# Decay tiles loaded as two 64-partition transfers, with new planner costs and due times, in a fused chunked-scan and gated-FFN kernel

## The chip, the cores and the metric

The kernel runs on one core of a Trainium2 chip. The metric is the time of one execution in device microseconds. Five engines work side by side, each through its own queue in order: TensorE (PE, with its weight loads shown apart as PEld), VectorE (DVE), ScalarE (ACT), GpSimd (POOL) and SyncE (SP). Here SP only issues transfers: each DMA instruction on its queue starts a transfer between HBM and the on-chip memories, and the transfers are carried by 16 DMA engines.

## The reference

A state-space scan in chunks, followed by a gated feed-forward layer over its output:

```python
# x: (4 batches, 8 heads, 768 steps, 32); a: (4, 8, 768); B, C: (4, 8, 768, 16)
for c in range(nc):                       # chunks of the sequence
    la  = log(clip(a, 1e-6, 1))[chunk];  cum = cumsum(la)
    L   = exp(cum_i - cum_j) for i >= j, else 0
    CB  = C_i . B_j
    y   = (CB * L) @ x  +  (C @ state) * exp(cum)
    state = exp(sum(la)) * state + sum_j exp(cum_last - cum_j) * B_j x_j^T
x2 = y as (3072 tokens, 256)
out = (sigmoid(x2 @ w_gate) * (x2 @ w_val)) @ w_out      # 256 -> 1536 -> 256
```

## The kernel before, in words

The sequence is cut into six chunks of 128 steps (c = 0 to 5), each worked as two halves of 64. A *unit* is one chunk of one batch (b = 0 to 3), so there are 24 units, numbered u = 4c + b, and they are worked two at a time from c = 1 on. When the four units of a chunk are done, its 512 tokens go through the feed-forward layer: 12 blocks f of 128 hidden columns, each a gate product `pg` and a value product `pv` (`gate`, `value`), then four output products `po` (`proj`). Chunk 0 uses the weights whole, in fp32; for chunks 1 to 5 the weights (18 tiles `w0` to `w17`) and the activations are each split into a rounded high part and a low part, and three products of parts stand for one.

What a unit does, by the names in the profile:

- `bn`, `cn`, `xn`: its B, C and x. Two transposes `pt` on PE give `bct`.
- `ab`, 128 partitions x 512 columns: its decays. Partition rows 0 to 63 all hold the same 512 values, those of the first half of the chunk (8 heads x 64 steps), and rows 64 to 127 those of the second half. They come out of a DRAM scratch `a_z`, in which the clipped `a` was saved with the first step of each half set to zero (`save_z`, L853). From c = 1 on `load_a` (L267) fetches them; a scan on DVE (L409, `decays`) turns them into the products of decays. In chunk 0 they are spread by PE instead (L569, `spread`).
- `pp`: the running products of `a`, from a second scratch `a_p` (`load_p`, L273).
- `weigh` (L468) multiplies the products C.B in PSUM (`pcb`, made by `multiply`, L454) by the decays and gives `m`; `within` (L480, L487) multiplies `m` by x; the state goes on through `ml`, `sm` (L522), `mr`, `sn` (L441) on DVE, and PE adds the part of the earlier state (L531). ACT and DVE then store the output of the unit as two parts `xh` and `xl` (L545, L551), which is the input of the feed-forward products.

All this is written as some 250 *tasks*, and a planner in the kernel (`run`, L176) sets the order of the instructions on every engine before anything is run. Each task is a chain of steps; each step names its engine, a cost in microseconds, what it needs and what it makes. The planner keeps a model clock for each engine, one for what the code calls the port, which every POOL step and the DVE steps marked `port=True` hold in turn, and for transfers a model of eight lanes, a fixed latency and a transfer time. At each turn it takes, among the steps that could start soonest, the one whose task has the earliest due time. Due times are formulas, overridden for single tasks by the table `DUES`. The plan fixes only the order on each queue; on the chip an instruction waits until what it needs is there, and everything behind it on its engine waits too. Eight transfers may be under way at a time: a ninth on SP waits for the one eight before it.

In the plan a decay transfer costs one issue of 0.52 us and 0.95 us on the transfer engines (L870). In the program the SP queue runs strictly in order through loads, decays and output stores alike. Six `ab` tiles exist (`NDEC`), so the load of unit u waits until unit u - 6 has been weighed.

Of the kernel before, what the change touches and what calls it, by code (L numbers as in the profile page):

```python
# [15 lines left out]
DRAM = bass.MemoryType.DRAM  # L16

DUES = {
# [16 lines left out]
}  # L35
WARM = 3

# [34 lines left out]
def tile_ssd_then_gated_ffn(  # L72
# [11 lines left out]
    nc = tc.nc  # L84
    NB, H, S, D = x.shape
# [5 lines left out]
    L2 = L // 2  # L91
# [6 lines left out]
    NDEC = 6  # L98
# [73 lines left out]
    def step(eng, cost, needs=(), makes=(), port=False, **buffers):  # L172

        return eng, cost, needs, makes, port, buffers
# [91 lines left out]

    def load_a(c, b):  # L267
        t = ld.tile([P, H, L2], F32, tag="ab", name=f"ab{c}_{b}", bufs=NDEC)
        src = a_z[2 * c : 2 * c + 2, b * H : (b + 1) * H].rearrange("i (o h) l -> i o (h l)", o=1)
        nc.sync.dma_start(t.rearrange("p h l -> p (h l)"), src.broadcast_to([2, L2, H * L2]))  # L270
        got["a", c * NB + b] = t

    def load_p(c, b):  # L273
# [81 lines left out]
    class Unit:  # L355
# [80 lines left out]
        def state(self):  # L436

            u = self.u
            yield step("dve", 0.22, [("after", u), ("first", u), ("p0",)], [("S", u)])
            states[u] = state_of(u, "sn")  # L440
            nc.vector.scalar_tensor_tensor(  # L441
                out=states[u], in0=self.s1, scalar=self.last(1), in1=self.after, op0=ALU.mult, op1=ALU.add
            )
# [14 lines left out]
    def multiply_after(*us):  # L458

        then = [u + 2 for u in us]  # L460
        yield step("pe", 0.65, [("bct", u) for u in then], [("cb", u) for u in then], cb=1)
        pcb = ps_cb.tile([P, NQ, 512], F32, tag="pcb", name=f"pcb{then[0]}")
        multiply(pcb, 0, *(units[u] for u in then))

# [35 lines left out]
    def results(*two):  # L500

        us = [t.u for t in two]
        n = len(two)
        c, more = two[0].c, two[0].more
        for t, u in zip(two, us):
            yield step("dve", 0.70, [("cb", u), ("scan", u), ("y", u - 4)], [("mult", u)])
            weigh(t)
        needs = [(k, u) for u in us for k in ("xn", "bdec")]
        yield step("pe", 0.2 + 0.37 * n, needs, [("y", u) for u in us])
        py = two[0].banks[:, :, 2 * L :].rearrange("p (i k) (s u l) -> p i k s u l", i=2, s=2, l=L2)  # L510
        for k, t in enumerate(two):
            within(
                t, lambda i, kt, rows: py[rows, i, kt, 0, k], lambda i, rows: py[rows, i, 0, 1, k], lambda kt: k == 0, more
            )

        yield step("dve", 0.25, [("first", u - 2) for u in us])
        ml = wk.tile([P, n, NG * D], F32, tag="ml", name=f"ml{two[0].nm}")
        chosen(ml, py[:, 0, 0, 1], n)
        for k, (t, u) in enumerate(zip(two, us)):
            yield step("dve", 0.22, [("S", u - NB), ("pp", u), ("inter", u - NB)], [("first", u)])  # L520
            t.s1 = state_of(u, "sm")
            nc.vector.scalar_tensor_tensor(  # L522
                out=t.s1, in0=states[u - NB], scalar=t.last(0), in1=ml[:, k], op0=ALU.mult, op1=ALU.add
            )
        yield step("pe", 0.2 + 0.23 * n, [("cd", u) for u in us], [("inter", u) for u in us])
        for k, t in enumerate(two):
            s0 = states.pop(t.u - NB)
            for i, state in enumerate((s0, t.s1)):
                for q in range(NQ):
                    qs, rows = slice(32 * q, 32 * q + 32), slice(64 * (q % 2), 64 * (q % 2) + 64)  # L530
                    nc.tensor.matmul(  # L531
                        py[rows, i, q // 2, 0, k], state[qs], t.cd[qs, i * L2 : (i + 1) * L2],
                        start=False, stop=True, skip_group_check=True,
                    )

        bs = two[0].b * L
        for i in range(2):
            yield step("act", ACT_HALF, [("gv", c - 2)])
            if two[0].b == 0 and i == 0:
                xb[c] = [wk.tile([P, NK, 512], F32R, tag=f"x{p}", name=f"x{p}{c}") for p in "hl"]  # L540
            hi, lo = (
                x[:, :, bs : bs + n * L].rearrange("p k (u i l) -> p k u i l", u=n, i=2)[:, :, :, i] for x in xb[c]
            )
            y = py[:, i, :, 0]
            nc.scalar.copy(hi, y)  # L545
            end = {"cb": -1} if i and not more else {}
            made = [("x", c, t.b) for t in two] if i else []
            if i and not more:
                made += [(k, u) for u in us for k in ("lo", "S", "after")]
            yield step("dve", DVE_HALF, [], made, **end)  # L550
            nc.vector.tensor_tensor(out=lo, in0=y, in1=hi.bitcast(F32), op=ALU.subtract)  # L551
        if more:
            yield step("dve", 0.25, [("S", u - 2) for u in us], [(k, u) for u in us for k in ("lo", "after")], cb=-1)
            ml = wk.tile([P, n, NG * D], F32, tag="mr", name=f"mr{two[0].nm}")
            chosen(ml, py[:, 1, 0, 1], n)
            for k, t in enumerate(two):
                t.after = ml[:, k]
# [194 lines left out]
    def proj(k, j):  # L752
# [3 lines left out]
        for f in range(NF):  # L756
            if f % 4 == 0:
                needs = [("h", k, f + i) for i in range(4)]
                needs += [("whole" if k == 0 else "w", NF + f // 2 + i) for i in range(2)]
                if f == 0 and k == 0:  # L760
                    needs.append(("gv", 0))
                yield step(
                    "pe", 0.92 if last else PROJ_T / 3 if k else 1.8, needs,
                    [("proj", k)] if j == NB - 1 and f + 4 == NF else [], banks=int(f == 0),
                )
                if f == 0:
                    acc = ps_mm.tile([P, 512], F32, tag="mm", name=f"po{k}_{j}")
# [13 lines left out]
        o = wk.tile([P, DM], F32, tag="o", name=f"o{k}_{j}")  # L781
# [61 lines left out]
    def load(n, transfer, needs, makes, fn):  # L843

        yield step("sp", 0.52 * n, needs, makes, transfer)
        fn()
# [20 lines left out]
    def decays_of(c, b):  # L867
        u = c * NB + b
        return {
            "a": load(1, 0.95, [("mult", u - NDEC), ("bdec", u - NDEC), ("a_z",)], [("a", u)], lambda: load_a(c, b)),  # L870
            "p": load(1, 0.3, [("cd", u - NPRE), ("S", u - NPRE), ("a_p",)], [("pp", u)], lambda: load_p(c, b)),
        }

# [61 lines left out]
    t = P0  # L935
# [45 lines left out]
```

## Time and profile before

| | us |
|---|---|
| median of three runs | 426.74 (426.37 to 427.24) |
| profiled execution, its own time | 427.21 |
| its span, first to last instruction | 425.4 |
| PE busy | 378.3 (89%) |
| DVE / ACT / POOL busy | 173.3 / 150.4 / 146.8 |
| mean granted TensorE clock | 0.939 |

The page of the profile gives busy times of each engine and cuts the span into 40 slices of 10.6 us. "PEclk" is the granted clock of TensorE: 9 in a slice is full speed, 5 is half. "DMA" is the mean share of the 16 DMA engines that was busy, so that one engine alone would show 0.06. The chain of waits is followed back from the last instruction; "DMA ab<-a_z" in it is time in which nothing but the landing of a decay tile was waited for.

### The profile page before, as it was taken

The numbers are of one execution on the slowest core, as the hardware profiler recorded it, in microseconds if no ns is written. First come the engines' busy times: TensorE is split into PE (matmuls) and PEld (weight loads), VectorE is DVE, ScalarE is ACT, GpSimd is POOL, SyncE is SP. The second block draws the span as 40 slices with busy tenths as digits, with TensorE's granted clock in tenths as the row PEclk, the third lists the DMA queues.
The fourth block names the chain that finished last, engine by engine and source line by source line (L and its number), as shares of the span: only waits on it lengthen the run. The fifth ranks groups of instructions, "written<-read, shape, count | busy, mean of one in ns | idle before, by whom it ended". The sixth has DMA issues, their size and how long they took to land.

```text
span 425.4 us, 7987 instructions
## 1 busy us (share of the span) xinstructions
PE 378.3 (89%) x3312; PEld 287.0 (67%) x3312; DVE 173.3 (41%) x298; ACT 150.4 (35%) x317; POOL 146.8 (35%) x159
## 2 busy tenths in 40 slices
PE   8899998036999899881999999999999999999997
PEld 3574444034776687771877778777888788888886
DVE  6679862067263427342253521664212421122211
ACT  2655572012342474302342402543315342144410
POOL 4535342012252697300344300543303343024420
PEclk9589999559899899997899999999999999999999
DMA  8999811114572301241702110410000000000001
GB/s 146 220 386 288 98 52 51 49 32 68 85 105 66 33 2 37 71 86 47 85 26 63 35 51 28 63 34 3 2 25 25 3 0 2 25 25 2 0 14 38
DMA packets 88670, 26.27 MB, mean 62 GB/s; under 512 B 75706, under 2 KB 81402, under 8 KB 88634
## 3 DMA queue, kind: packets, MB, share of 16 engines
q1 hardware_dynamic: 88634, 25.76, 27.1%
q8 instruction: 26, 0.43, 0.5%
q14 instruction: 10, 0.08, 0.1%
HBM read 22.41 MB, written 3.34 MB: 61 GB/s over the span
## 4 chain that ended last, share of the span: by engine, by line
PE 61%; DMA 26%; SPq 6%; DVE 4%; issue 2%; ACT 1%; DVEq 0%; ACTq 0%
DMA ab<-a_z 18%; PE pv L746 16%; PE pg L746 16%; PE po L779 8%; PE po L780 4%; SPq L270 4%; PE po L769 4%; DMA out_dram<-o 3%; DMA cn<-in_C_dram 3%; PE pg L737 2%; PE pv L737 2%; PE pcb L480 1%; DMA wr<-in_moe_w_gate_dram 1%; DVE m L468 1%; PE pcb L454 1%
## 5 line engine op out<-in xcount | busy, mean ns | idle before, releaser
L708 POOL TENSOR_TENSOR h<-g,h 128x512 fp32r<-128x512 f32 x60 | 77.5, 1291 | 148.7 <-ACT h L706 144.7
L746 PE MATMUL pg<-xh,w 128*128 128x512 f32 x240 | 86.2, 400 | 2.6 <-DVE g L702 2.6
L746 PE MATMUL pv<-xh,w 128*128 128x512 f32 x240 | 87.3, 405 | 0.0
L779 PE MATMUL po<-w,h 128*128 128x512 f32 x228 | 81.8, 401 | 2.2 <-DVE o L794 2.2
L702 DVE TENSOR_TENSOR g<-pv,g 128x512 f32<-128x512 f32 x60 | 41.4, 690 | 90.3 <-PE pv L746 89.0
L706 ACT CAST h<-g 128x512 fp32r<-128x512 f32 x60 | 37.2, 621 | 78.4 <-DVE g L702 78.4
L780 PE MATMUL po<-w,h 128*128 128x256 f32 x228 | 64.0, 281 | 0.0
L746 PEld LDWEIGHTS pg<-xh,w 128*128 128x128 f32 x240 | 45.3, 189 | 14.3 <-DVE g L702 3.5
L746 PEld LDWEIGHTS pv<-xh,w 128*128 128x128 f32 x240 | 46.1, 192 | 10.2 <-issue 0.3
L679 ACT ACTIVATE g<-pg 128x512 f32<-128x512 f32 x72 | 43.1, 598 | 27.7 <-PE pg L746 16.7
L409 DVE TENSOR_TENSOR_SCAN ab<-ab,delta 128x512 f32<-128x512 f32 x20 | 25.4, 1278 | 66.2 <-DMA ab<-a_z 66.2
L779 PEld LDWEIGHTS po<-w,h 128*128 128x128 f32 x228 | 42.8, 188 | 13.4 <-DVE o L794 2.8
L746 PE MATMUL pv<-xl,w 128*128 128x512 f32 x120 | 47.7, 398 | 0.0
L746 PE MATMUL pg<-xl,w 128*128 128x512 f32 x120 | 47.0, 391 | 0.0
L780 PEld LDWEIGHTS po<-w,h 128*128 128x128 f32 x228 | 43.1, 189 | 0.3
L792 ACT COPY o<-po 128x256 f32<-128x256 f32 x20 | 7.5, 374 | 76.7 <-PE po L780 60.3
L321 POOL TENSOR_TENSOR wr<-wr 128x512 int32<-128x512 int32 x18 | 21.0, 1173 | 28.6 <-ACT wr L319 26.8
L334 POOL TENSOR_TENSOR w<-wr,w 128x512 fp32r<-128x512 f32 x18 | 24.2, 1346 | 14.1 <-ACT w L332 11.7
L794 DVE TENSOR_TENSOR o<-po,o 128x256 f32<-128x256 f32 x20 | 8.2, 420 | 50.9 <-ACT o L792 50.9
L480 PE MATMUL pcb<-m,xn 64*32 64x64 f32 x640 | 11.0, 241 | 18.8 <-DVE m L468 18.8
L769 PE MATMUL po<-wr,h 128*128 128x256 f32 x96 | 26.6, 430 | 0.0
L746 PEld LDWEIGHTS pv<-xl,w 128*128 128x128 f32 x120 | 23.1, 193 | 4.4
(103 smaller groups left out, 441.2 us busy)
## 6 DMA issues: line engine op xcount, KB each, us to landing
ab<-a_z SPq DMA_DIRECT2D x20, 256.0 KB
wr<-in_moe_w_gate_dram SPq DMA_DIRECT2D x6, 512.0 KB
wr<-in_moe_w_val_dram SPq DMA_DIRECT2D x6, 512.0 KB
wr<-in_moe_w_out_dram SPq DMA_DIRECT2D x6, 512.0 KB
out_dram<-o SPq DMA_DIRECT2D x24, 128.0 KB
xn<-in_x_dram SPq DMA_DIRECT2D x10, 256.0 KB
bn<-in_B_dram SPq DMA_DIRECT2D x10, 128.0 KB
cn<-in_C_dram SPq DMA_DIRECT2D x10, 128.0 KB
```

The lines of the kernel that those rows point to most:

```text
L270: nc.sync.dma_start(t.rearrange("p h l -> p (h l)"), src.broadcast_to([2, L2, H * L2]))
L321: nc.gpsimd.tensor_tensor(out=lw.bitcast(I32), in0=hw.bitcast(I32), in1=lw.bitcast(I32), op=ALU.add)
L334: engines[eng].tensor_tensor(out=lo, in0=lw, in1=hi.bitcast(F32), op=ALU.subtract)
L409: nc.vector.tensor_tensor_scan(out=t.rearrange("p h l -> p (h l)"), data0=t.rearrange("p h l -> p (h l)"), data1=delta.rearrange("p h l -> ...
L679: nc.scalar.activation(gs[k, f], pm, AF.Sigmoid)
L702: nc.vector.tensor_tensor(out=g, in0=pm, in1=g, op=ALU.mult)
L706: copies[eng](hh, g)
L708: engines[eng].tensor_tensor(out=hl, in0=g, in1=hh.bitcast(F32), op=ALU.subtract)
L746: nc.tensor.matmul(pm, w[:, part, kt, fs], xx[:, kt], start=(i == 0), stop=(i == 3 * NK - 1))
L769: nc.tensor.matmul(acc[:, :DM], hs[k, f][:, js], whole[NF + f // 2][:, f % 2], start=(f == 0), stop=(f == NF - 1))
L779: nc.tensor.matmul(acc, hh, w.rearrange("p i m -> p (i m)"), start=(f == 0), stop=False, skip_group_check=True)
L780: nc.tensor.matmul(acc[:, :DM], hl, w[:, 0, :], start=False, stop=(f == NF - 1), skip_group_check=True)
```

## The change

Three things change.

1. `load_a` issues two transfers in place of one. Before, one transfer wrote all 128 partitions, from a source pattern of 2 halves x 64 repeats x 512 values. Now each half has a transfer of its own, from a source pattern of 64 repeats x 512 values onto 64 partitions. The bytes are the same: 256 KB for a unit.
2. Costs in the plan: a decay load counts two issues; the small state updates `sm` and `sn` go from 0.22 to 0.24 us and now hold the shared port; three groups of small products on PE get longer costs; and the output products j = 2 and 3 of every chunk now need the last value product of their chunk.
3. A new table `DUES`, and with it another order on every engine.

No arithmetic changes: the engines get the same instructions as before, but for 20 more DMA issues on SP.

```diff
 DUES = {
-    "ap": -143.9, "b0": -890.9, "x0": -647.8, "b1": -735.7, "b2": -249.4, "x2": -91.9, "w0": -1118.8, "w2": -303.1,
...
+    "b0": -655.8, "x0": -471.1, "b1": -574.7, "x1": -470.2, "b2": -319, "w0": -1049, "b3": -401.9, "w1": -369.8,
...
 }
     def load_a(c, b):
         t = ld.tile([P, H, L2], F32, tag="ab", name=f"ab{c}_{b}", bufs=NDEC)
-        src = a_z[2 * c : 2 * c + 2, b * H : (b + 1) * H].rearrange("i (o h) l -> i o (h l)", o=1)
-        nc.sync.dma_start(t.rearrange("p h l -> p (h l)"), src.broadcast_to([2, L2, H * L2]))
+        for i in range(2):
+            src = a_z[2 * c + i, b * H : (b + 1) * H].rearrange("(o h) l -> o (h l)", o=1)
+            nc.sync.dma_start(
+                t[i * L2 : (i + 1) * L2].rearrange("p h l -> p (h l)"), src.broadcast_to([L2, H * L2])
+            )
         got["a", c * NB + b] = t
...
-            yield step("dve", 0.22, [("after", u), ("first", u), ("p0",)], [("S", u)])
+            yield step("dve", 0.24, [("after", u), ("first", u), ("p0",)], [("S", u)], port=True)
...
-        yield step("pe", 0.65, [("bct", u) for u in then], [("cb", u) for u in then], cb=1)
+        yield step("pe", 0.8, [("bct", u) for u in then], [("cb", u) for u in then], cb=1)
...
-        yield step("pe", 0.2 + 0.37 * n, needs, [("y", u) for u in us])
+        yield step("pe", 0.2 + 0.45 * n, needs, [("y", u) for u in us])
...
-            yield step("dve", 0.22, [("S", u - NB), ("pp", u), ("inter", u - NB)], [("first", u)])
+            yield step("dve", 0.24, [("S", u - NB), ("pp", u), ("inter", u - NB)], [("first", u)], port=True)
...
-        yield step("pe", 0.2 + 0.23 * n, [("cd", u) for u in us], [("inter", u) for u in us])
+        yield step("pe", 0.2 + 0.3 * n, [("cd", u) for u in us], [("inter", u) for u in us])
...
-                if f == 0 and k == 0:
-                    needs.append(("gv", 0))
+                if f == 0 and (k == 0 or j > 1):
+                    needs.append(("gv", k))
...
-            "a": load(1, 0.95, [("mult", u - NDEC), ("bdec", u - NDEC), ("a_z",)], [("a", u)], lambda: load_a(c, b)),
+            "a": load(2, 0.95, [("mult", u - NDEC), ("bdec", u - NDEC), ("a_z",)], [("a", u)], lambda: load_a(c, b)),
```

At the start of the program the weight tiles `w1`, `w11` and `w3` are now issued on SP ahead of the x of units 2 and 3; before, of the weights only `w0` and `w2` were. How the change moves the instructions further on, at three places. Names carry chunk and batch (`ab1_0` is the decay tile of chunk 1, batch 0; `h0_11` is hidden block 11 of chunk 0; `wr15` is a weight tile as it was loaded).

SP, the first decay loads, after the scratch tensors have been written. Before:

```order
L276 DMA pp2_0_658<-a_p_110 128x1x128
L270 DMA ab1_1_661<-a_z_109 128x1x512
L270 DMA ab1_2_671<-a_z_109 128x1x512
L270 DMA ab1_3_675<-a_z_109 128x1x512
L270 DMA ab2_0_678<-a_z_109 128x1x512
L270 DMA ab2_1_686<-a_z_109 128x1x512
L270 DMA ab1_0_694<-a_z_109 128x1x512
L270 DMA ab2_2_788<-a_z_109 128x1x512
L270 DMA ab2_3_796<-a_z_109 128x1x512
L258 DMA bn2_0_799<-in_B_dram 128x16x16
L258 DMA cn2_0_801<-in_C_dram 128x16x16
L265 DMA xn2_0_862<-in_x_dram 128x16x32
```

The same place with the change:

```order
L302 DMA wr15_576<-in_moe_w_out_dram 128x2x512
L275 DMA ab1_3_629<-a_z_109 64x512 x2
L275 DMA ab2_0_634<-a_z_109 64x512 x2
L275 DMA ab1_1_645<-a_z_109 64x512 x2
L283 DMA pp1_0_665<-a_p_110 128x1x128
L283 DMA pp1_1_676<-a_p_110 128x1x128
L283 DMA pp1_2_686<-a_p_110 128x1x128
L283 DMA pp1_3_689<-a_p_110 128x1x128
L283 DMA pp2_0_697<-a_p_110 128x1x128
L275 DMA ab1_0_699<-a_z_109 64x512 x2
L275 DMA ab1_2_708<-a_z_109 64x512 x2
L275 DMA ab2_1_720<-a_z_109 64x512 x2
```

Each decay tile is now two rows. The tile that is used first, `ab1_0`, was the sixth decay tile on the queue and is now the fourth; three decay tiles stand ahead of the `pp` loads instead of behind them.

DVE, at the end of the first feed-forward pass, where the first scans of chunk 1 stand. Before:

```order
L409 SCALAR_TENSOR_TENSOR ab1_1_661<-ab1_1_661,delta_99 128x512
L308 TENSOR_SCALAR wt14_733<-wt14_733 128x512
L700 TENSOR_TENSOR h0_9_743<-pv0_9_725,g0_9_718 128x512
L310 TENSOR_SCALAR wt14_733<-wt14_733 128x512
L700 TENSOR_TENSOR h0_10_757<-pv0_10_747,g0_10_750 128x512
L315 SCALAR_TENSOR_TENSOR wr14_447<-wr14_447,wt14_733 128x512
L308 TENSOR_SCALAR wt15_745<-wt15_745 128x512
L409 SCALAR_TENSOR_TENSOR ab1_0_694<-ab1_0_694,delta_99 128x512
L468 TENSOR_TENSOR m1_0_772<-pcb1_1_701,ab1_0_694 128x512
L700 TENSOR_TENSOR h0_11_780<-pv0_11_763,g0_11_770 128x512
```

With the change:

```order
L416 SCALAR_TENSOR_TENSOR ab2_1_720<-ab2_1_720,delta_99 128x512
L707 TENSOR_TENSOR h0_9_760<-pv0_9_738,g0_9_741 128x512
L315 TENSOR_SCALAR wt15_749<-wt15_749 128x512
L315 TENSOR_SCALAR wt14_706<-wt14_706 128x512
L317 TENSOR_SCALAR wt15_749<-wt15_749 128x512
L707 TENSOR_TENSOR h0_10_773<-pv0_10_762,g0_10_765 128x512
L322 SCALAR_TENSOR_TENSOR wr15_576<-wr15_576,wt15_749 128x512
L317 TENSOR_SCALAR wt14_706<-wt14_706 128x512
L416 SCALAR_TENSOR_TENSOR ab1_0_699<-ab1_0_699,delta_99 128x512
L475 TENSOR_TENSOR m1_0_795<-pcb1_1_592,ab1_0_699 128x512
L707 TENSOR_TENSOR h0_11_798<-pv0_11_780,g0_11_788 128x512
```

The scan of `ab1_0` stands where it stood, ahead of the last hidden block `h0_11`; a scan of a chunk-2 tile, `ab2_1`, has come in ahead of it.

PE, where the output products of chunk 0 end and the feed-forward pass of chunk 1 begins. Before:

```order
L374 MATMUL pt2_2_1103<-eye_88,bn2_1_990 128x128
L375 MATMUL pt2_2_1103<-eye_88,cn2_1_992 128x128
L769 MATMUL po0_3_1055<-wr16_478,h0_8_692 128x256
L769 MATMUL po0_3_1055<-wr16_478,h0_9_743 128x256
L769 MATMUL po0_3_1055<-wr17_487,h0_10_757 128x256
L769 MATMUL po0_3_1055<-wr17_487,h0_11_780 128x256
L454 MATMUL pcb8_1128<-bct2_0_954 64x128 x8
L454 MATMUL pcb8_1128<-bct2_1_971 64x128 x8
L746 MATMUL pg1_0_1147<-xh1_901,w0_275 128x512
```

With the change:

```order
L381 MATMUL pt2_0_1104<-eye_88,bn2_0_806 128x128
L382 MATMUL pt2_0_1104<-eye_88,cn2_0_808 128x128
L776 MATMUL po0_3_1060<-wr16_473,h0_8_745 128x256
L776 MATMUL po0_3_1060<-wr16_473,h0_9_760 128x256
L776 MATMUL po0_3_1060<-wr17_555,h0_10_773 128x256
L776 MATMUL po0_3_1060<-wr17_555,h0_11_798 128x256
L753 MATMUL pg1_0_1133<-xh1_923,w0_204 128x512
```

The transposes of units 9 and 10 and the products `pcb8` of the first pair of chunk 2 no longer stand ahead of the first gate product of chunk 1; `pcb8` now follows the third pair of gate and value products. The transpose of unit 8 alone is left ahead of it.

34 rows, old and new, of the table DUES are left out of this document.

## The prediction

> **What bounds the kernel now.** I read the shares of the engines first, then the busy time by stage, then who PE waited for.
>
> ```profile
> PE 378.3 (89%) x3312; PEld 287.0 (67%) x3312; DVE 173.3 (41%) x298; ACT 150.4 (35%) x317; POOL 146.8 (35%) x159
> PE 61%; DMA 26%; SPq 6%; DVE 4%; issue 2%; ACT 1%; DVEq 0%; ACTq 0%
> ```
>
> PE is busy 89% of the span, and no other engine half of it. But a quarter of the chain that ended last is DMA. The stages (stretch, width, busy time of PE, PEld, DVE, ACT and POOL, then granted clock, DMA share, GB/s) say where PE lacks work:
>
> ```profile
> 0.00:27.20 27.20, 23.44 (x309) 13.23 (x310) 17.38 (x44) 12.19 (x35) 11.54 (x24) 0.75 0.92 227
> 27.20:69.00 41.80, 41.80 (x140) 20.51 (x140) 33.26 (x52) 25.15 (x49) 19.77 (x20) 1.00 0.64 161
> 69.00:92.00 23.00, 4.16 (x50) 3.20 (x49) 3.60 (x6) 0.00 (x0) 0.82 (x2) 0.66 0.11 41
> 92.00:126.00 34.00, 29.95 (x404) 23.17 (x386) 18.46 (x32) 11.50 (x29) 12.49 (x14) 0.88 0.54 84
> 126.00:162.00 36.00, 33.37 (x259) 26.16 (x257) 15.12 (x23) 17.94 (x35) 22.15 (x23) 0.95 0.18 32
> 162.00:184.00 22.00, 20.11 (x281) 16.25 (x280) 12.38 (x17) 7.40 (x18) 11.21 (x13) 1.00 0.23 60
> 184.00:212.00 28.00, 17.56 (x166) 14.16 (x166) 7.14 (x14) 5.98 (x16) 3.85 (x5) 0.82 0.49 77
> 212.00:262.00 50.00, 47.50 (x433) 38.39 (x432) 19.83 (x35) 14.37 (x27) 14.46 (x14) 1.00 0.14 41
> 262.00:422.00 160.00, 160.00 (x1303) 131.71 (x1301) 45.75 (x80) 55.92 (x110) 50.51 (x46) 1.00 0.07 17
> ```
>
> From 27 to 69 us (feed-forward pass of chunk 0) and from 262 to 422 (the last chunks) PE has no idle time. Between 69 and 262 it lacks 18.84 + 4.05 + 2.63 + 1.89 + 10.44 + 2.50 = 40.35 us (width less PE busy, six rows). Who made it wait:
>
> ```profile
> DVE ab L409 <- DMA ab<-a_z: 66.2, 13, 21.0
> PE pcb L480 <- DVE m L468: 18.8, 1, 18.8
> PE pt L374 <- ACT bct L389: 9.2, 1, 9.2
> ACT o L792 <- DMA out_dram<-o: 15.8, 1, 15.8
> 68.69 19.65 DMA ab<-a_z
> 94.71 11.91 DMA cn<-in_C_dram
> 125.34 12.93 DMA ab<-a_z
> 184.85 1.51 SPq L270 DMA_DIRECT2D ab<-a_z  x2
> 186.45 12.36 DMA out_dram<-o
> ```
>
> All four large waits lead to the decay transfer. PE's 18.8 us (72.7 to 91.5) is for `m`, which waits for the scan, which waits 21.0 us for `ab`. PE's 9.2 us before 200.6 is for ACT, which could not write `o` because an output store took 12.36 us to land: it was issued right behind two decay tiles. The load of `cn` behind decay tiles took 11.91 us, and PE lost 4 us for it. So decay tiles are slow, and they slow what is issued after them. Why they are slow, in a stretch in which they alone were moving (69 to 88 us):
>
> ```profile
> q1 hardware_dynamic: 458, 0.92, 12.9%
> ab<-a_z SPq DMA_DIRECT2D x1, 256.0 KB
> 20.00:30.00 10.00, 9.27 (x141) 7.66 (x134) 7.38 (x21) 4.78 (x12) 3.27 (x3) 0.74 1.04 380
> ```
>
> 12.9% of 16 engines is 2.06: a decay tile runs on two DMA engines, while the weight loads of 20 to 30 us fill all 16 (share 1.04, 380 GB/s). A packet takes 19 x 16 x 0.129 / 458 = 0.0856 us, and a tile of 256 KB is 128 packets of 2 KB, 64 for each engine, 5.5 us. Two source halves, two engines: the pattern of 2 x 64 x 512 was divided by its outer 2.
>
> One more cost hangs on the stalls, the clock:
>
> ```profile
> 91.50:97.00 5.50, 5.43 (x106) 4.34 (x106) 5.18 (x12) 1.24 (x2) 1.04 (x1) 0.50 0.32 58
> 107.10:110.50 3.40, 3.40 (x11) 2.62 (x10) 0.00 (x0) 0.89 (x3) 1.20 (x3) 0.52 0.25 57
> 137.90:140.20 2.30, 0.25 (x2) 0.04 (x1) 1.90 (x3) 0.06 (x1) 0.00 (x0) 1.00 0.08 12
> 141.30:144.70 3.40, 3.40 (x10) 2.62 (x9) 0.69 (x1) 1.84 (x5) 3.40 (x5) 0.51 0.10 10
> 200.60:206.10 5.50, 5.47 (x107) 4.29 (x108) 1.54 (x5) 1.14 (x4) 0.82 (x2) 0.50 0.77 112
> 142.13 2.56 PE pv L746 x6
> 148.88 1.36 PE pv L746 x6
> ```
>
> After each stall PE works for 3.4 to 5.5 us at half clock, where a group of six matmuls takes 2.56 us (part of it at half) against 1.36. The four rows at about 0.50 hold 5.43 + 3.40 + 3.40 + 5.47 = 17.70 us of work, half of it lost: 8.85 us.
>
> **The change, part by part.** *The transfer.* Each half now has 64 rows as its outer dimension. If that dimension is what is shared out, as the 2 was, a half runs on 16 engines with 4 packets each: 0.34 us, both halves 0.7 in place of 5.5. What else a tile costs is read from one that was issued with no other decay tile ahead:
>
> ```profile
> 106.24 0.50 SPq L270 DMA_DIRECT2D ab<-a_z  x1
> 113.69 2.34 DVE L409 TENSOR_TENSOR_SCAN ab<-ab,delta 128x512 f32<-128x512 f32 x2 [7.63 <-DMA ab<-a_z]
> ```
>
> From issue to scan 7.45 us; less 0.5 of issue and 5.5 of packets leaves 1.45 us of landing. New: two issues, 0.34 for the last half, 1.45: about 2.8 us. Bounds: 2.3 (if the halves overlap fully), and 7.5 or more (if nothing spreads; a rival below). I take 2.8, since the weight loads do fill 16 engines.
>
> The Trainium skill, DMA: Bandwidth & Descriptors, section Rules for kernel authors, speaks against such a split: two transfers to disjoint partition halves serialize, because both halves already use all 16 engines, and one transfer of 128 partitions should be used. The row above, two engines busy, shows that its reason does not hold for this tile; by the rule the time would stay at 426.7. The same page, section Why a DMA increments its semaphore by 16 and not by 1, gives the engine count as the largest number up to 16 that divides the outermost dimension larger than 1 on both sides: 2 before, which the trace agrees with, and 16 after, which no run here shows yet. By that the sum below stands.
>
> *Twenty more issues on SP*, 0.51 us each by the second row here, 10 us in all:
>
> ```profile
> 46.75 3.42 DMA a_p<-a
> L270 SPq DMA_DIRECT2D ab<-a_z x20: 482/507/5662, 53.5 to 239.1; - x20
> SPq L803 <- DVE o L794: 162.0, 15, 42.7
> 110.54 5.53 PE po L769 x24
> ```
>
> SP waits 162 us for finished outputs alone, so this costs nothing while the loads run ahead. The tight place is the first batch: six tiles and five `pp`, 17 issues, some 9 us, from about 50 us (46.75 + 3.42, where a scratch tensor landed before; their order among the weight loads moves, the bytes before them don't). The sixth lands at about 62. PE first needs `m1_0` after eight `po` matmuls of chunk 0, two records of 0.23 us each: 69 + 3.7 = 72.7. Without that cover each issue would cost its 0.51.
>
> *Costs and due times.* No instruction is added, so they are worth only what the new order makes wait. Up to 69 us I take no change: PE is full from 27.2 on, and before that the same work of the first units stands in nearly the same order; the x of units 2 and 3 now comes behind three more weight tiles of 0.5 MB (1.4 us each at 380 GB/s), and PE reaches those units late enough. Ends: 2 us better, 4 worse. After 69 the work of the helpers is squeezed. The stretch of 69 to 212 us loses 37.85 us of idle and 8.85 of clock and becomes 96 us. In its five rows DVE is busy 56.7 us, POOL 50.5 and ACT 42.8: 59%, 53% and 45% of 96. Enough on average; what is late next is the chain of each pair of units on DVE (`m`, `ml`, `sm`, `xl`, `mr`), which must fit between two groups of PE work. Small waits of that kind stand in the trace now:
>
> ```profile
> PE pcb L454 <- DVE mr L495: 1.9, 2, 1.2
> PE pcb L531 <- DVE ml L495: 0.9, 1, 0.9
> PE pcb L531 <- DVE sm L522: 0.7, 1, 0.7
> ```
>
> I keep all three, 3.5 us. Ends: nothing, or the rival with stalls below.
>
> **The sum**, against the profiled execution: span 425.4 - 40.35 of idle - 8.85 of clock = 376.2; + 3.5 of small waits = 379.7. Median less span is 426.74 - 425.4 = 1.34 (the profiled execution's own 427.21 lies 1.8 above its span, within the runs shown). Forecast **381.0 us**, faster by 45.7 (10.7%).
>
> **The rivals.**
>
> *New stalls in the squeezed stretch.* DVE or POOL falls behind, because a scan or a weight part is due where a chunk's products are. For it: POOL was busy 22.15 of 36 us between 126 and 162 while the weight parts and hidden blocks shared it, and that work now meets the units earlier. Against: PE was full in most of that stretch all the same. Price of one: the gap of 137.9 to 140.2 was 2.05 us of idle, and the 3.4 us at half clock right after it cost 1.7 more: 3.75. Three to six: 381 + 11 to 22, 392 to 403.
>
> The Trainium skill, TensorE: Matmul & The Clock Gate, section HAM oscillation, has it that only PE-idle gaps longer than about 3.4 us bring the half clock. The trace differs: a gap of 2.05 us was followed by it. By the page three stalls would end at 387.
>
> *The transfers stay on two engines*, or one after the other: the split does nothing. Then the waits for decays stay, moved a little by the new order: about 427. Against it is the share of 2.06 engines, which fits the outer 2 so well.
>
> *Slower.* The source of a half repeats one row 64 times. If that repeated dimension is not counted, each half is one row long for the sharing and runs on one engine, and both halves on the same one: 128 x 0.0856 = 11 us a tile. Place: the first eight tiles, from 53 us on, take 88 us and not 44. Price: up to 44 us there, 447 to 471 in all; later pairs need 22 us each, about what PE has between two pairs (twelve groups of 1.36 us, half of a chunk's output products and the units), so they stay nearly hidden. It decides from 5.5 us a tile on. Against it: the repeats were dimension two of the old pattern and its two engines show the outer one being used.
>
> **How the numbers follow.** Forecast 0.72, its own range 375 to 388 (2 us better at the start and no small waits, or two stalls more). New stalls 0.20. Two engines 0.03. Slower 0.05. About 0.2% is what a measurement of this kernel can tell from no change. Forecast and stalls are both faster, with 0.01 of the two-engine case: 0.93; the same 0.01; slower 0.05 + 0.01 = 0.06. The range that leaves out no more than 2 in 10 takes the forecast's case and most of the stalls: 375 to 395.
>
> **What would show it.** Right: packets of `ab` on all 16 engines, tile landing within 3 us, no wait of DVE on `ab` above 1 us; no 12 us store or `cn`; PE idle between 69 and the end of chunk 3 under 5 us and no half clock after 30 us; the first gate product of chunk 1 at about 95 us (69 + 22 of `po` + 4 of units). Wrong: `ab` still in the chain of waits (transfer), PE waiting on DVE or POOL for several gaps of 2 us (order), or the first pass starting after 30 us (loads).

## The result, and the profile after

The changed kernel takes 378.51 us (median of four runs, 377.68 to 380.74) against 426.56 us before: a ratio of 0.8881, with a 95% interval of 0.8841 to 0.8921. The forecast was 381.0. The profiled execution took 378.78 us, with a span of 377.0.

The page of the changed kernel, its shares of the engines, its chain of waits, the scans and the issues of decay transfers (count, size of one, median time to landing):

```profile
PE 367.3 (97%) x3312; PEld 280.6 (74%) x3312; DVE 167.9 (45%) x298; ACT 149.4 (40%) x317; POOL 150.6 (40%) x159
PE 92%; DMA 3%; SPq 2%; DVE 1%; ACT 0%; issue 0%; POOL 0%; POOLq 0%
L416 DVE TENSOR_TENSOR_SCAN ab<-ab,delta 128x512 f32<-128x512 f32 x20 | 25.4, 1281 | 3.0 <-DMA ab<-a_z 3.0
ab<-a_z SPq DMA_DIRECT2D x40, 128.0 KB, 3.1
```

DMA was 26% of the chain and is 3%. All twenty scans together wait 3.0 us for their tiles, where they waited 66.2. The same stretches as before, in the same columns:

```profile
0.00:27.20 27.20, 22.62 (x307) 12.60 (x308) 18.41 (x44) 12.56 (x35) 13.68 (x26) 0.81 0.83 160
27.20:69.00 41.80, 39.95 (x137) 19.67 (x137) 32.10 (x52) 23.99 (x49) 17.79 (x19) 1.00 0.80 227
69.00:92.00 23.00, 23.00 (x335) 17.45 (x334) 17.08 (x31) 6.67 (x13) 11.18 (x12) 1.00 0.50 73
92.00:126.00 34.00, 34.00 (x330) 27.16 (x329) 16.72 (x27) 18.13 (x41) 21.60 (x22) 1.00 0.45 81
126.00:162.00 36.00, 36.00 (x469) 29.54 (x470) 16.25 (x28) 14.79 (x36) 18.21 (x21) 1.00 0.34 72
162.00:184.00 22.00, 22.00 (x300) 17.16 (x293) 14.77 (x25) 10.56 (x23) 10.66 (x11) 1.00 0.46 72
184.00:212.00 28.00, 28.00 (x146) 23.81 (x145) 6.98 (x10) 6.69 (x13) 6.82 (x5) 1.00 0.10 29
212.00:262.00 50.00, 50.00 (x504) 40.85 (x503) 16.48 (x34) 18.52 (x37) 18.00 (x18) 1.00 0.18 32
262.00:374.00 112.00, 111.71 (x810) 92.40 (x808) 28.98 (x49) 37.49 (x74) 32.68 (x28) 1.00 0.03 11
```

From 69 to 262 us PE is busy in every stretch for its whole width, at full clock: the 40.35 us of idle time and the half clock of that part are gone. What is left lies in the first two rows. PE lacks 4.58 + 1.85 = 6.43 us there, where it lacked 3.76 before. The clock of the first row rose from 0.75 to 0.81: 13.6 us at half clock became 10.3 (twice the missing share of 27.2 us), worth at most 1.6 us of PE's work. The start is therefore about one microsecond worse in this execution, and the rest is better by what the stalls cost. Summed: 425.4 + 2.67 - 1.6 - 40.35 - 8.85 + 0.29 (idle time after 262) = 377.6, against a measured span of 377.0.

### The profile page after: what moved, and what is told of

Its sections match the earlier page's. It is cut to its first block, busy times and chain, and to the rows that moved or that the text cites. A ratio compares the mean times of both kernels' runs of the same rounds, so it can differ in the third digit from the quotient of the medians.

```text
span 377.0 us, 8030 instructions
## 1 busy us (share of the span) xinstructions
PE 367.3 (97%) x3312; PEld 280.6 (74%) x3312; DVE 167.9 (45%) x298; ACT 149.4 (40%) x317; POOL 150.6 (40%) x159
## 4 chain that ended last, share of the span: by engine, by line
PE 92%; DMA 3%; SPq 2%; DVE 1%; ACT 0%; issue 0%; POOL 0%; POOLq 0%
PE pg L753 22%; PE pv L753 22%; PE po L786 14%; PE po L787 7%; PE po L776 6%; PE pv L744 5%; PE pg L744 5%; PE pcb L487 2%; SPq L262 2%; PE pcb L461 2%; PE pcb L538 2%; DMA wr<-in_moe_w_gate_dram 2%; DMA wr<-in_moe_w_val_dram 1%; PE pcb L494 1%; PE pt L381 1%; PE po L783 1%
## 5 line engine op out<-in xcount | busy, mean ns | idle before, releaser
L753 PE MATMUL pv<-xh,w 128*128 128x512 f32 x240 | 85.2, 396 | 0.0
L753 PEld LDWEIGHTS pv<-xh,w 128*128 128x128 f32 x240 | 45.1, 188 | 9.8 <-ACT w L339 0.2
L753 PE MATMUL pv<-xl,w 128*128 128x512 f32 x120 | 46.8, 390 | 0.0
L328 POOL TENSOR_TENSOR wr<-wr 128x512 int32<-128x512 int32 x18 | 19.4, 1082 | 27.2 <-ACT wr L326 22.2
L341 POOL TENSOR_TENSOR w<-wr,w 128x512 fp32r<-128x512 f32 x18 | 25.7, 1428 | 11.2 <-ACT w L339 11.1
L426 POOL TENSOR_TENSOR bd<-bn,ab 128x128 f32<-128x128 f32 x24 | 11.3, 476 | 37.6 <-PE pcb L494 33.0
L753 PEld LDWEIGHTS pg<-xl,w 128*128 128x128 f32 x120 | 22.6, 188 | 4.1
```

Source lines behind the costliest of these rows:

```text
L328: nc.gpsimd.tensor_tensor(out=lw.bitcast(I32), in0=hw.bitcast(I32), in1=lw.bitcast(I32), op=ALU.add)
L341: engines[eng].tensor_tensor(out=lo, in0=lw, in1=hi.bitcast(F32), op=ALU.subtract)
L753: nc.tensor.matmul(pm, w[:, part, kt, fs], xx[:, kt], start=(i == 0), stop=(i == 3 * NK - 1))
```

## The experiments

Four kernels take the change apart; then four more settle what the first left open. In each group all kernels ran on one chip beside the kernel before, which took 425.87 us in the first group and 426.88 in the second.

**The new order with the old transfer.** The changed kernel, in which `load_a` issues one transfer again:

```diff
-        for i in range(2):
-            src = a_z[2 * c + i, b * H : (b + 1) * H].rearrange("(o h) l -> o (h l)", o=1)
-            nc.sync.dma_start(
-                t[i * L2 : (i + 1) * L2].rearrange("p h l -> p (h l)"), src.broadcast_to([L2, H * L2])
-            )
+        src = a_z[2 * c : 2 * c + 2, b * H : (b + 1) * H].rearrange("i (o h) l -> i o (h l)", o=1)
+        nc.sync.dma_start(t.rearrange("p h l -> p (h l)"), src.broadcast_to([2, L2, H * L2]))
```

> The changed kernel with one thing undone: each unit's decays come again as one transfer with an outer dimension of 2; costs, due times and so the order on every engine stay those of the change. Theory (a tile sits on two DMA engines, 5.5 us each, and the change's gain is the 16 engines): decay tiles take over 5 us each again, DVE waits for them for tens of us, the share of the DMA engines beside them is about 0.13, and the time is over 400 us. The sixth tile of the first batch would land at about 48.7 + 33 + 1.5 = 83 us, and the new order puts its scan ahead of the last hidden blocks of chunk 0, so PE should stall there by some 20 us. Rival (the new order and costs bring the gain, the split little): within 2% of the changed kernel's 378.5, under 386 us.

Measured: 439.51 us, 1.0324 of before (1.0266 to 1.0382). So with the old transfer the new costs and due times make the kernel slower. Two of its waits (us in total, times, the longest), one of DVE and one of PE:

```profile
DVE ab L413 <- DMA ab<-a_z: 74.1, 10, 15.8
PE pg L741 <- DVE h L704: 21.8, 2, 11.3
```

PE's wait is in the pass of chunk 0 (L741 is its gate product) and comes to 21.8 us. What DVE did there, in order of time (start, us, what, idle time before it and its cause):

```profile
71.74 1.23 DVE L413 TENSOR_TENSOR_SCAN ab<-ab,delta 128x512 f32<-128x512 f32 x1 [12.49 <-DMA ab<-a_z]
...
89.90 1.23 DVE L413 TENSOR_TENSOR_SCAN ab<-ab,delta 128x512 f32<-128x512 f32 x1 [15.76 <-DMA ab<-a_z]
91.04 0.67 DVE L704 TENSOR_TENSOR h<-pv,g 128x512 f32<-128x512 f32 x1
```

These are the scan of `ab1_1` ahead of `h0_8` and that of `ab2_1` ahead of `h0_9`. On the queue these tiles are now the third and the sixth decay tile; in the old order the first scan was of the first tile on the queue. With tiles that come one after the other from two engines, DVE stood 28 us for scans that nobody needed yet, and PE for the hidden blocks behind them.

**The split alone.** The kernel before, its plan and its order, with the two transfers:

```diff
-        src = a_z[2 * c : 2 * c + 2, b * H : (b + 1) * H].rearrange("i (o h) l -> i o (h l)", o=1)
-        nc.sync.dma_start(t.rearrange("p h l -> p (h l)"), src.broadcast_to([2, L2, H * L2]))
+        for i in range(2):
+            src = a_z[2 * c + i, b * H : (b + 1) * H].rearrange("(o h) l -> o (h l)", o=1)
+            nc.sync.dma_start(
+                t[i * L2 : (i + 1) * L2].rearrange("p h l -> p (h l)"), src.broadcast_to([L2, H * L2])
+            )
```

> The kernel before with the split alone: two transfers of 64 partitions, while costs, due times and the order on every engine stay those of before (only the decay issue on SP is doubled). Theory: the 40.35 us of PE idle between 69 and 262 us and the 8.85 us of half clock go, so 425.4 - 49.2 = 376.2 of span, 377.5 us without small waits, 377 to 384 with up to 6 us of them. Rival (an order planned for 0.95 us per tile with one issue is still wrong, and the new due times bring half of the gain or more): over 400 us.

Measured: 377.86 us, 0.888 of before (0.8841 to 0.8919). The whole gain is there without any new cost or due time. Its page and three of its stretches:

```profile
PE 95%; SPq 1%; DVE 1%; DMA 1%; ACT 0%; issue 0%
L412 DVE TENSOR_TENSOR_SCAN ab<-ab,delta 128x512 f32<-128x512 f32 x20 | 28.4, 1434 | 1.5 <-DMA ab<-a_z 1.5
```

```profile
27.20:69.00 41.80, 41.80 (x140) 20.46 (x139) 34.47 (x53) 24.72 (x47) 19.39 (x21) 1.00 0.72 181
69.00:92.00 23.00, 23.00 (x369) 18.19 (x371) 17.67 (x29) 7.94 (x20) 10.87 (x13) 1.00 0.56 90
126.00:162.00 36.00, 35.38 (x448) 29.22 (x447) 21.56 (x33) 14.36 (x35) 17.25 (x20) 1.00 0.49 92
```

The old order has no idle time of PE between 27 and 126 us, and 0.62 us between 126 and 162, all that PE waits for after 69 us:

```profile
PE pcb L534 <- DVE sm L525: 0.6, 1, 0.6
```

Its helpers kept up in the squeezed stretch as well.

**Two transfers, two engines.** The changed kernel, with the source of each half written as 2 x 32 x 512 in place of 64 x 512 (the reshape of the source gets a dimension of one more):

```diff
-                t[i * L2 : (i + 1) * L2].rearrange("p h l -> p (h l)"), src.broadcast_to([L2, H * L2])
+                t[i * L2 : (i + 1) * L2].rearrange("p h l -> p (h l)"), src.broadcast_to([2, L2 // 2, H * L2])
```

> The changed kernel with two transfers of 64 partitions for each tile, but each from a source pattern of 2 x 32 x 512 values in place of 64 x 512. Theory (the outer dimension sets the number of DMA engines): each half runs on two engines, 32 packets for each, and the tile takes 5.5 us as before; the time is that of the one-transfer version, over 400 us, and the DMA share beside the decays is about 0.13. Rival (two transfers in place of one are what helps, whatever their pattern, for instance by landing separately): about 378 us.

Measured: 442.56 us, 1.0386 of before (1.0343 to 1.0429), as slow as one transfer. Here are the waits and one stretch of it:

```profile
DVE ab L416 <- DMA ab<-a_z: 80.6, 10, 15.7
```

```profile
69.00:92.00 23.00, 6.25 (x8) 2.38 (x8) 4.26 (x6) 2.05 (x5) 3.59 (x5) 0.57 0.12 44
```

The DMA share of 0.12 in a stretch where little else moves is two engines of 16. Same bytes, same two transfers, same order as the changed kernel; only the outer count differs. So it is not the number of transfers that counts, but the pattern that each of them carries.

**Four engines.** The same edit with 4 x 16 x 512 (`broadcast_to([4, L2 // 4, H * L2])`).

> The changed kernel with each half from a source pattern of 4 x 16 x 512 values. Theory: four engines, 16 packets of 0.0856 us for each half, 2.7 us for a tile. The sixth tile lands at about 48.7 + 16.4 + 1.5 = 67 us, some us after its scan's turn, and all later tiles in time: 379 to 388 us, between the changed kernel and the version on two engines, and much nearer to the former. Rival (only the full 16 engines help): over 400 us.

Measured: 393.88 us, 0.9242 of before (0.9208 to 0.9275), above what was expected. Stretches of 3.4 us of this kernel, the columns as above:

```profile
66.09:69.51 3.42, 1.53 (x4) 0.39 (x2) 0.00 (x0) 0.51 (x1) 0.25 (x1) 1.00 0.26 97
69.51:72.92 3.41, 0.00 (x0) 0.00 (x0) 1.23 (x2) 0.00 (x0) 0.00 (x0) 1.00 0.11 40
72.92:76.33 3.41, 2.78 (x4) 1.23 (x5) 3.41 (x8) 0.60 (x2) 0.00 (x0) 0.50 0.00 0
76.33:79.75 3.42, 3.42 (x6) 1.35 (x5) 1.53 (x2) 1.78 (x4) 1.82 (x3) 0.50 0.04 4
```

A DMA share of 0.26 is four engines: the outer counts 2 and 4 gave two and four. A stretch of the changed kernel (outer count 64) in which only decay tiles moved:

```profile
109.80:111.30 1.50, 1.50 (x70) 1.05 (x72) 0.48 (x1) 0.79 (x3) 1.18 (x2) 1.00 0.82 173
```

0.82 is 13 of 16 engines at work on average; no such stretch shows all 16 busy throughout.

The price of a tile on four engines was expected rightly: 256 KB at 97 GB/s is 2.7 us. The start was not, and neither was what followed. This is the chain that ended last around the stall (start, us, what):

```profile
63.10 8.56 DMA ab<-a_z
...
71.72 1.11 issue
72.83 0.68 DVE h L707
```

The second half of the sixth tile, `ab2_1`, was issued at 62.5 to 63.1 us and landed at 71.7, not at 67. The expectation let the six tiles move from 48.7 us on; the weight tiles issued just ahead of them still filled the engines until 52:

```profile
50.00:52.00 2.00, 2.00 (x7) 0.84 (x6) 1.97 (x4) 0.60 (x2) 0.89 (x1) 1.00 0.99 375
52.00:54.00 2.00, 2.00 (x6) 0.97 (x5) 1.64 (x3) 1.78 (x3) 0.21 (x1) 1.00 0.41 144
```

The scan of `ab2_1` stands ahead of `h0_9`, PE waited 5.9 us for that block, and two stretches at half clock followed. Nor did all later tiles come in time: between 184 and 212 us PE lacks another 2.48 us, behind scans that waited for their tiles, with one more stretch at half clock. PE lacks 7.8 us more than in the changed kernel, and three stretches of 3.41 us at half clock cost up to 5.1: 12.9 of the 13.7 us by which the spans differ. The expectation had no term for the clock.

**The start.** The changed kernel lost time before 30 us. The chain there:

```profile
22.93 5.88 DMA wr<-in_moe_w_gate_dram
28.84 0.66 ACT wt L313
29.49 0.33 ACT xh L637 x2
29.87 1.14 PE pg L733 x4
```

ACT waits for the weight tile `w4`, and the copies `xh` of unit 3, for which PE waited 1.8 us, stand behind it. In the next kernel the order is that of the changed kernel, taken from a list, with one move: the first four steps on `w4` come behind those copies and the first sigmoid `g0_0`. On ACT:

```diff
-L313 ACTIVATE wt4
 L637 COPY xh0 <- py0_3
 L637 COPY xh0 <- mm0_3
 L686 ACTIVATE g0_0
+L313 ACTIVATE wt4
```

> The changed kernel with one task moved: the four steps that make the first parts of weight tile w4 (wt4 on ScalarE, three small steps on VectorE) come behind the copies xh of unit 3 and the sigmoid g0_0 instead of ahead of them; everything else in the order is as it was. Theory (the start lost its time because ScalarE waited for w4 from DRAM with the copies queued behind it, and TensorE waited 1.8 us for those copies): that wait of TensorE goes, the first pass ends up to 1.8 us earlier, 376.2 to 377.6 us against 378.5 of the changed kernel. Rival (the start is bound by the arrival of the weights, and the wait only moves to the next tile): 378.0 to 379.0, with a wait of TensorE of the same size a little later.

Measured: 378.66 us (378.22 to 379.54). The changed kernel in the same group took 378.18 (377.89 to 379.08). The long wait went and the time stayed. ACT and PE in this kernel, in order of time:

```profile
27.20 0.27 ACT L637 COPY xh<-py 128x128 f32<-128x128 f32 x1 [0.50 <-DVE wide L616]
28.64 0.27 ACT L637 COPY xh<-mm 128x128 f32<-128x128 f32 x1 [1.17 <-PE mm L622]
...
28.95 1.14 PE L733 MATMUL pg<-xh,wr 128*128 128x256 f32 x4 [0.36 <-ACT xh L637]
34.86 1.96 PE L744 MATMUL pg<-xh,wr 128*128 128x512 f32 x4 [0.24 <-ACT g L686]
```

The same gate products in the changed kernel of this group:

```profile
29.04 1.14 PE L733 MATMUL pg<-xh,wr 128*128 128x256 f32 x4 [1.20 <-ACT xh L637]
34.54 1.88 PE L744 MATMUL pg<-xh,wr 128*128 128x512 f32 x4
```

The copies no longer wait for `w4`, but the second one now waits for its own input, the product `mm` of unit 3, which PE finished just before 28.6 us. So the gate product starts 0.09 us earlier and no more. The next one that could show a gain starts 0.32 us later: 0.24 us of it is a wait for a sigmoid that stands behind the tile `w5` in both kernels, and that tile was taken up 0.33 us later here. (One trace of each; the unit products ahead of these rows ran some 0.4 us later in this one.) My theory is wrong here: the wait for `w4` hid a chain of unit 3 (`wide` on DVE, `mm` on PE, `xh` on ACT) that ends at nearly the same time. The rival had the time right, and its reason (the wait moves to the next tile) only for those 0.24 us. What a start without either would give was not tried.

**Four transfers of 32 partitions.** Each tile as four transfers, 40 issues more on SP, order unchanged:

```diff
-        for i in range(2):
-            src = a_z[2 * c + i, b * H : (b + 1) * H].rearrange("(o h) l -> o (h l)", o=1)
+        for k in range(4):
+            src = a_z[2 * c + k // 2, b * H : (b + 1) * H].rearrange("(o h) l -> o (h l)", o=1)
             nc.sync.dma_start(
-                t[i * L2 : (i + 1) * L2].rearrange("p h l -> p (h l)"), src.broadcast_to([L2, H * L2])
+                t[k * L2 // 2 : (k + 1) * L2 // 2].rearrange("p h l -> p (h l)"), src.broadcast_to([L2 // 2, H * L2])
```

> The changed kernel with each decay tile as four transfers of 32 partitions (source 32 x 512), 40 issues on SyncE more; order unchanged. By the engine count each still spreads over 16 engines (32 rows). Theory (the issues are covered, since SyncE waits for outputs most of the time): 378.0 to 380.5 us, no wait of VectorE on ab above 2 us. Rival (each issue lies on the path, or eight transfers under way are too few): 40 x 0.51 = 20 us at most, 382 to 399.

Measured: 380.35 us (379.04 to 381.42), 2.2 above the changed kernel in the same group. The scans of this kernel:

```profile
L416 DVE TENSOR_TENSOR_SCAN ab<-ab,delta 128x512 f32<-128x512 f32 x20 | 26.7, 1337 | 13.6 <-DMA ab<-a_z 13.0
```

The time is within what was expected, the wait is not: DVE waits 13.0 us in all for its tiles, where it waits 3.0 in the changed kernel, and the longest wait is 5.8 us. Of PE's waits only 0.3 us, for a hidden block, lie behind them. So 40 issues cost about 2.2 us by the medians and not 20; where these 2.2 lie the profile doesn't settle.

**The split alone, and the changed kernel, once more.**

> The kernel before with the split in load_a alone, once more, beside the changed kernel. Theory (costs and due times bring nothing that can be measured): 377 to 378.5 us and within 0.3% of the changed kernel. Rival (the new order costs the 1.4 us by which the spans differed): at least 0.3% faster than the changed kernel.

> The changed kernel itself, for comparison within one chip and call: 377.7 to 379.5 us.

Measured: 377.75 us (376.12 to 379.57) for the split alone, 378.18 (377.89 to 379.08) for the changed kernel. The medians are 0.11% apart and the runs overlap, so costs and due times bring nothing that can be measured with fast decay tiles. The rival's 0.3% was not seen.

## Why the prediction was right

**The transfer.** "If that dimension is what is shared out, as the 2 was" holds: outer 2, 4 and 64 gave 442.56, 393.88 and 378.51 us in the same order of work, and the split alone, in the old order, gave the whole gain. The Trainium skill, DMA: Bandwidth & Descriptors, section Why a DMA increments its semaphore by 16 and not by 1, gives these engine counts, and the shares of 0.12 and 0.26 agree. Its advice in the section Rules for kernel authors against two transfers to partition halves, and with it 426.7 us, did not apply here: its reason is that both halves use all 16 engines, so that nothing is gained over one transfer that does so too, and the one transfer of the kernel before used two (share 0.129).

The landing of a tile was sized too small. It was forecast at 2.8 us for both halves: two issues, 0.34 us of packets for the last half, 1.45 us of landing. Measured, one half takes a median of 3.1 us from the start of its own issue, and an issue 0.59, so a tile takes about 3.7 us (an estimate from these two medians); the longest half took 7.4, in the first batch, where twelve transfers queue. Part of the difference is in the row of the changed kernel at 109.80 us: at a share of 0.82 and 173 GB/s a packet of 2 KB takes 0.155 us (0.82 x 16 x 2048 bytes / 173 GB/s), where 0.0856 was taken over from the two engines. A later stretch with decay tiles alone, 184.2 to 185.7 us, has 0.58 and 168 GB/s, which is 0.113 us. "Tile landing within 3 us" was missed, and so was "no wait of DVE on `ab` above 1 us": there are two waits, 2.0 us the longest. Neither cost PE anything, because the tiles are fetched well ahead; this error had no place in the sum.

The two-engine rival and the slower rival with one engine for each half are excluded by the times and by the shares (the lower end of the latter, 447 us, has no working in the prediction).

**The stalls and the clock.** Both terms, 40.35 and 8.85 us, came as forecast: PE has no wait left between 69 and 262 us, and no half clock after the start. No output store takes longer than 3.5 us to land, and no `cn` longer than 5.7. One reading was loose: of the 4 us put down to `cn`, 2.4 were a wait for `bn`, the load just ahead of it, and 1.7 for `cn`; both went with the slow tiles, so the term stands.

**The small waits** were sized at 3.5 us and measured at nothing. This term failed: the chain of `m`, `ml`, `sm`, `xl`, `mr` on DVE fits between groups of PE work in the new order, and in the old one too, but for 0.6 us. With it fell the rival of new stalls in the squeezed stretch. Since the old order with fast tiles keeps 0.6 us of such waits, the others in the trace before hung on the late decays and not on a lack of time on DVE. The prediction had counted them as waits that stay.

**The start** was taken as no change, with ends of 2 us better and 4 worse. It is about 1 us worse, the second term that was off; moving the copies ahead of `w4` did not bring it back. In the second trace of the changed kernel it is 0.7 us worse, without any change of the clock there. The split alone, in the old order, lost nothing at the start: PE lacks 3.20 us before 69 us, against 3.76 before and 6.43 and 4.47 in the two traces of the changed kernel. By these traces the loss belongs to the new order. PE is full from 29.9 us on, not from 27.2, just short of the 30 us that was named as a sign of being wrong. The two errors, 3.5 too many and 1 too few, have opposite signs and together make up the 2.5 us between forecast and median; that the forecast is this close is in part luck, because one offsets some of the other.

**The order.** "They are worth only what the new order makes wait" was right, but the prediction didn't say how much hangs on it: with the old transfer the new order costs 3%, because a scan that is not urgent was placed ahead of the last hidden blocks. And one mark was missed: the first gate product of chunk 1 started at 98.1 us, not at about 95:

```profile
L776 PE MATMUL po<-wr,h x96: 385/388/493, 71.2 to 98.1; 128*128 128x256 f32 x96
L753 PEld LDWEIGHTS pg<-xh,w x240: 186/188/190, 98.1 to 354.8; 128*128 128x128 f32 x120
```

The pass of chunk 0 ended at 71.2 us, not at 69 (first and last start stand in each row). How much of this is the start, and how much work that now stands ahead, was not separated. From there on the 22 us of products and 4 of units took 26.9.

## What to carry to other kernels

When a transfer is slow, divide the busy share of the DMA engines in a stretch where it moves alone by 1/16: if the number of engines equals the count of the pattern's outermost dimension, reorder or split the pattern so that this count is large (32 and 64 were tried here), before anything else is tuned. Don't expect the rate to grow with the count all the way: two engines moved the tiles at 49 GB/s (69 to 88 us of the kernel before), four at 97, and the tiles of the changed kernel went at 173 in the row at 109.80 us, 3.5 times two engines and not eight. Why was not tested. A new order of work should be judged on the kernel that it will run in: due times that were harmless with fast tiles cost 3% with slow ones. In an in-order queue the operation to check is the first one that can be late, not the first one that is needed.

## What the hardware showed

In every trace of this case the granted clock changes on a grid of 3.41 us. Two places of the kernel before and one of the kernel with sources of 2 x 32 x 512, cut along that grid (columns as above):

```profile
103.82:107.23 3.41, 0.89 (x4) 0.67 (x5) 2.21 (x3) 0.14 (x1) 0.00 (x0) 1.00 1.01 124
107.23:110.65 3.42, 3.42 (x10) 2.63 (x10) 0.00 (x0) 0.76 (x3) 1.20 (x3) 0.50 0.22 55
...
137.95:141.37 3.42, 1.37 (x6) 1.03 (x6) 3.01 (x4) 1.23 (x3) 0.53 (x1) 1.00 0.05 8
141.37:144.78 3.41, 3.41 (x9) 2.63 (x9) 0.61 (x1) 1.77 (x5) 3.41 (x5) 0.50 0.13 12
144.78:148.19 3.41, 3.41 (x16) 2.80 (x16) 1.25 (x2) 1.76 (x3) 2.78 (x3) 1.00 0.80 84
```

```profile
185.48:188.90 3.42, 1.53 (x37) 1.30 (x38) 2.94 (x8) 0.37 (x1) 0.00 (x0) 1.00 0.84 105
188.90:192.31 3.41, 3.41 (x12) 2.86 (x11) 1.58 (x3) 0.37 (x1) 0.00 (x0) 0.50 0.20 52
```

In these rows the busy time of one window goes with the clock of the next. After windows with PE busy for 0.89, 1.37 and 1.53 us the next one ran at half clock; after the 1.53 at 66.09 us with four engines it did not. So the border lies at about 1.5 us of 3.41 here, and one window busy throughout brought the full clock back each time. In the start of the changed kernel the border is another:

```profile
11.96:15.37 3.41, 2.13 (x76) 1.25 (x83) 2.27 (x5) 1.93 (x8) 1.92 (x3) 1.00 1.06 275
15.37:18.79 3.42, 2.95 (x38) 1.82 (x38) 3.41 (x9) 2.98 (x10) 2.06 (x4) 0.50 0.64 180
18.79:22.20 3.41, 2.08 (x60) 1.66 (x52) 2.15 (x5) 1.34 (x4) 2.40 (x4) 0.50 1.02 235
```

Here 2.13 us of busy time brought the half clock and 2.95 us did not end it. Most matmuls of this part use 32 or 64 rows of the array and not 128; whether that is the cause was not tested.

The Trainium skill, TensorE: Matmul & The Clock Gate, Part 1: The HAM clock gate, names a free-running window of 3413 ns, and these rows agree with it; they differ from its statement that the half clock comes after at least one idle window: windows with PE busy for 0.89 to 1.53 us were enough. By the rows, the price in the prediction is explained: the 2.05 us of idle fell into one window and cost the next one 3.4 us at half clock.
